# Experts' numbers, the first long list's rows and their preparation one step sooner, in a kernel of attention and two expert layers

## Chip, core and metric

One Trainium2 chip, one core. The metric is the device time of one execution in microseconds (us). An execution was also profiled; all rows below come from that one.

## What is computed

Clustered attention, then two expert layers on its output. The change lies in the first expert layer:

```
logits = x @ w_gate;  noisy = logits + log1p(exp(x @ w_noise)) * noise
top2 = two largest of 8 experts per token;  top2_w = softmax over the two
for e in range(8):
    for k in range(2):
        mask = top2[:, k] == e
        h = maximum(x[mask] @ w1[e], 0)
        out[mask] += top2_w[mask, k] * (h @ w2[e])
```

There are 1536 tokens of 512 numbers; w1 is 512 x 1024 and w2 is 1024 x 512 for each expert. All is float32 in the reference.

## The kernel before, in words

**Lists and jobs.** While attention runs, the tokens of every expert are written by indexed DMA into a list in HBM (`xg`). Experts 0 and 1 have two short lists each (256 rows, 240 of them used), one for each half of the batch; experts 2 to 7 have one long list each. Ten jobs work these lists off: jobs 0 and 1 are the short lists of the first half, jobs 2 to 7 the long lists from the fullest to the emptiest, jobs 8 and 9 the short lists of the second half. Which expert stands behind job 2 is known only at run time: `Dp.ranks`, called in step 6, sorts the six experts on VectorE (DVE) and leaves their numbers in `permi` (line 793).

**Steps.** A job has 8 steps, one for each 128 of the 1024 hidden numbers, so there are 80 steps; step s is job s // 8. Job 2, the first long list, begins with step 16. For step s:

- `load_w(s)` (lines 949 to 956): one DMA of 512 KB, issued by SyncE (SP), brings the weights of the step into one of four places `WR[s % 4]`.
- `split_hi(s)` (line 959) on ScalarE (ACT) writes the rounded weights to `ring`; `split_lo(s)` (lines 961 to 968) writes what the rounding left, on DVE. In steps 13 to 15 DVE does the first half (line 966) and GpSimd (POOL) the second (line 968). There are three places in `ring`, so `split_hi(s)` waits until TensorE (PE) has done `second(s - 3)`.
- `first(s)` (line 1061): 12 matmuls, over the rounded weights times both parts of the rows, and the rest times the rounded rows. The third matmul is the first that reads what `split_lo` wrote. Then ACT (line 1066) and DVE (line 1067) take the result out as `H`, again in two parts.
- `second(s)` (line 1102, for long lists `second_t`, line 1129): the product with w2. It reads both parts of `H`.

**Rows of a job.** `load_x(j)` (lines 970 to 998) issues four DMAs for the rows (line 982) and a few for the weights of the tokens (lines 994 and 996). For a long list their addresses come from the expert's number, which `load_perm` (line 945) reads from `permi` into registers of SP, six reads for six experts. `prep_t` (line 1016, DVE) turns half a list's rows, `prep_h` (line 1023, ACT) rounds them, and `prep_l` (line 1029, DVE for job 2) keeps the rest. Job 2 is done in two halves.

**Order of the work.** The loop at lines 1841 to 1919 writes out the order of every queue by hand; each engine, and SP, does its instructions in that order. Step s issues, in this order: at s == LX the experts' numbers (`load_perm`), then `load_w(s + 5)`, at s == LX also `load_x(2)`; then `first(s + 1)`, `second(s)`, `split_hi(s + 3)` and `split_lo(s + 3)`, and the preparations that the table `prep` has for the step. In steps 12 to 15 (`soon`) the preparations stand ahead of the two splits, in all others behind them. In step 15, `second(15)` comes ahead of `first(16)`.

`PREP[j] = (s, n, engines)` gives the step in which the turning of the first part of job j begins, in how many parts it is done, and on which engine `prep_l` runs; `PH` and `PL` (1 and 1) say how many steps later `prep_h` and `prep_l` of a part follow. Below, hi 13, lo 13, first 13, second 13 and H 13 are the splits, matmuls and hidden numbers of step 13, w 13 is its DMA, and x 2 are the rows of job 2.

The lines of the loop that set SP's order:

```
if s == LX:
    while todo:
        gap(1000, 1000)
    M1.load_perm()
if 4 + len(SP) <= s + 5 < ns:
    M1.load_w(s + 5)
if s == LX:
    M1.load_x(2)
```

Of the kernel before, what the change touches and what calls it, by code (L numbers as in the profile page):

```python
# [44 lines left out]


OV = 24
PREP = {2: (12, 2, "dd"), 4: (2, 3, "ppp"), 8: (3, 2, "dd"), 9: (8, 2, "dd")}
LOADS = {-16: ("b0",), -14: ("a0",), -12: ("a1",), -10: ("a2",), -8: ("a3",), -6: ("x0", "x2"), -5: ("x4", "b2"), -4: ("b3",), -3: ("c0", "c1")}
B4, B5, B6 = 6, 6, 3  # L50
X9 = 57
# [1464 lines left out]
def body(tc, qk, q2, k2, v2, cent, wgn, noise, w12, phi, v12, out):  # L1516
    nc = tc.nc
    with ExitStack() as ctx:
# [152 lines left out]
        for i in range(Dp.NFILL):  # L1671
            at(ends, 2 * (i // 4) + 3, Dp.fill, i)

        LX = 9
        todo = []
        gates = [Dp.gate(q, *x) for q, x in enumerate(((0, 6), (6, 3), (9, 3)))]

# [154 lines left out]
        for j in range(2, len(M1.jobs)):  # L1832
            s, n, eng = PREP[j if j in PREP else 4]
            if j > 2:
# [6 lines left out]
        for s in range(ns):  # L1841
            j, f = M1.steps[s]
# [8 lines that stand above are left out]
# [127 lines left out]
```

## Time and profile before

| what | us |
|---|---|
| median of 3 runs | 622.95 |
| the 3 runs | 622.3, 622.95, 626.76 |
| the profiled execution, its time | 620.13 |
| its span, first to last instruction | 618.3 |

The span is what the views below show; 1.83 us of the profiled execution lie around it. Steps 0 to 15 run from about 234 to 289 us of the span, job 2 begins at 289.45 us. A row of the timeline gives the start, the duration, engine and line, operation and tiles, and in brackets how long the engine was idle before it and what ended that. SPq is SyncE's queue.

### The profile page before, as it was taken

What the parts mean: (1) busy time and instruction counts of PE and PEld (TensorE: products, weight loads), DVE (VectorE), ACT (ScalarE), POOL (GpSimd) and SP (SyncE); (2) the same over time, 40 slices, a digit from 0 to 9 for tenths busy, and PEclk for the clock granted to TensorE, in tenths of its full rate; (3) what the DMA queues carried; (4) which work ended last, traced back from release to release, by engine and by line L of the source; (5) the groups of instructions that cost most, each with busy time, mean ns of one, the idle gap of its engine ahead of it and who ended that gap; (6) DMA issues with size and microseconds to landing.
All of it is one profiled execution on the core that took longest, in us unless ns stands there. A gap on an engine that the chain in (4) does not pass through costs nothing. (4 is left out here: it accounts for less than half of the span.)

```text
span 618.3 us, 11612 instructions
## 1 busy us (share of the span) xinstructions
PE 595.7 (96%) x4241; PEld 480.5 (78%) x4241; DVE 419.3 (68%) x841; ACT 322.0 (52%) x467; POOL 292.5 (47%) x267
## 2 busy tenths in 40 slices
PE   8999999999999999798999999999999999997996
PEld 6666767666677668587999999999999888874544
DVE  6875788676776388466554958769595977644533
ACT  5877667676676663255344363644646375532002
POOL 3998788787989851634030160432616044220100
PEclk9999999999999999899999999999999999999999
DMA  8262474552357683788935559899997979989985
GB/s 326 74 234 77 149 278 162 214 190 107 129 180 250 225 256 143 251 184 251 193 102 143 153 122 228 352 207 337 285 308 160 299 204 345 308 267 335 426 364 204
DMA packets 59084, 139.43 MB, mean 225 GB/s; under 512 B 11504, under 2 KB 27056, under 8 KB 56976
## 3 DMA queue, kind: packets, MB, share of 16 engines
q1 hardware_dynamic: 53168, 125.31, 60.2%
q0 software_dynamic: 5856, 13.36, 10.2%
q8 instruction: 34, 0.56, 0.4%
q14 instruction: 26, 0.21, 0.1%
HBM read 108.18 MB, written 28.35 MB: 221 GB/s over the span
## 5 line engine op out<-in xcount | busy, mean ns | idle before, releaser
L966 DVE TENSOR_TENSOR ring<-wr,ring 128x1024 fp32r<-128x1024 f32 (+1 forms) x77 | 92.6, 1203 | 62.1 <-ACT ring L959 61.0
L959 ACT ACTIVATE ring<-wr 128x1024 fp32r<-128x1024 f32 x77 | 81.4, 1059 | 78.3 <-PE py L1129 47.3
L1129 PE MATMUL py<-H,ring 128*128 128x448 f32 (+5 forms) x480 | 97.7, 352 | 0.0
L1129 PEld LDWEIGHTS py<-H,ring 128*128 128x128 f32 x480 | 88.6, 188 | 2.6
L352 DVE TENSOR_REDUCE mp<-pmx 128x1 f32<-128x512 f32 x96 | 63.7, 684 | 12.7 <-PE pmx L347 12.3
L1066 ACT ACTIVATE H<-ph 128x240 fp32r<-128x240 f32 (+6 forms) x80 | 36.4, 455 | 68.7 <-PE ph L1061 56.2
L395 ACT ACTIVATE pts<-psc 128x768 f32<-128x768 f32 x72 | 57.9, 812 | 26.6 <-PE psc L391 22.8
L1061 PE MATMUL ph<-XS1a,ring 128*128 128x240 f32 (+3 forms) x288 | 67.9, 326 | 0.0
L1102 PE MATMUL py<-ring,H 128*128 128x512 f32 (+1 forms) x246 | 64.0, 398 | 2.4 <-DVE H L1067 1.3
L1061 PE MATMUL ph<-XS0a,ring 128*128 128x432 f32 (+3 forms) x252 | 63.8, 337 | 0.1
L1152 POOL DMA_INDIRECT x2acc<-y,mdi x20 | 33.4, 1668 | 61.4 <-ACT y L1171 25.5
L1067 DVE SCALAR_TENSOR_TENSOR H<-ph,H 128x240 fp32r<-128x240 f32 (+6 forms) x80 | 40.8, 510 | 24.9 <-ACT H L1066 17.2
L1102 PEld LDWEIGHTS py<-ring,H 128*128 128x128 f32 (+1 forms) x246 | 42.4, 183 | 12.4 <-DVE H L1067 2.5
L408 PE MATMUL pav<-pts,vt 128*64 128x384 f32 x288 | 51.7, 492 | 0.0
L428 POOL TENSOR_TENSOR psa<-psa,pts 128x768 f32<-128x768 f32 x27 | 49.7, 1840 | 3.5 <-ACT pts L395 1.9
L1061 PEld LDWEIGHTS ph<-XS1a,ring 128*128 128x128 f32 x288 | 47.8, 188 | 2.1 <-DVE ring L966 0.2
L1029 POOL TENSOR_TENSOR XS0b<-xr,XS0a 128x512 fp32r<-128x512 f32 (+1 forms) x9 | 17.0, 1888 | 67.9 <-ACT XS0a L1023 67.9
L1061 PE MATMUL ph<-XS0b,ring 128*128 128x240 f32 (+3 forms) x192 | 46.2, 312 | 1.2 <-DVE ring L966 0.8
L1061 PE MATMUL ph<-XS1b,ring 128*128 128x240 f32 (+3 forms) x192 | 46.3, 314 | 0.1
L1061 PEld LDWEIGHTS ph<-XS0a,ring 128*128 128x128 f32 x252 | 44.2, 195 | 1.8 <-issue 0.5
L1029 POOL TENSOR_TENSOR XS1b<-xr,XS1a 128x512 fp32r<-128x512 f32 (+1 forms) x6 | 11.4, 1906 | 54.5 <-ACT XS1a L1023 54.5
L408 PEld LDWEIGHTS pav<-pts,vt 128*64 128x64 f32 x288 | 19.2, 136 | 23.1 <-issue 21.1
(377 smaller groups left out, 1205.0 us busy)
## 6 DMA issues: line engine op xcount, KB each, us to landing
wr<-in_w SPq DMA_DIRECT2D x80, 512.0 KB
v<-in_v SPq DMA_DIRECT2D x9, 2048.0 KB
xg<-xr SPq DMA_DIRECT2D x14, 516.0 KB
wr<-in_qk SPq DMA_DIRECT2D x8, 768.0 KB
early<-in_q SPq DMA_DIRECT2D x8, 768.0 KB
early<-in_k SPq DMA_DIRECT2D x8, 768.0 KB
x2acc<-xr SPq DMA_DIRECT2D x8, 512.0 KB
vt<-in_v SPq DMA_DIRECT2D x8, 384.0 KB
```

The source lines that it names most:

```text
L352: nc.vector.tensor_reduce(mp[:, 0, col:col + 1], ps, axis=AX.X, op=OP.max)
L395: nc.scalar.activation(pt, ps[:, :, :384], AF.Exp, scale=SCALE)
L408: nc.tensor.matmul(self.avp[p, qh][64 * hh:64 * hh + 64, :384], self.vt[p][:, hh, kc, :], pt[:, hh, :], start=(kc == 0), stop=(kc == 5))
L428: eng.tensor_tensor(s, s, pt.pop((p, t)), op=OP.add)
L959: self.nc.scalar.activation(self.ring[s][0], self.wr[s], AF.Copy)
L966: nc.vector.tensor_tensor(lo[:, :n], wr[:, :n], f32(hi)[:, :n], op=OP.subtract)
L1061: nc.tensor.matmul(ph[:, :u], a[:, 128 * c:128 * c + 128], x[:, c, :u], start=(c == 0 and i == 0), stop=(c == 3 and i == 2))
L1066: nc.scalar.activation(HH[:, :u], ph[:, :u], AF.Relu)
L1067: nc.vector.scalar_tensor_tensor(HL[:, :u], ph[:, :u], 0.0, f32(HH)[:, :u], op0=OP.max, op1=OP.subtract)
L1102: nc.tensor.matmul(py, x, y, start=(f == 0 and i == 0), stop=(f == NF - 1 and i == 2))
L1129: nc.tensor.matmul(py[:, :w], a[:, k], x[:, :w], start=(f == 0 and i == 0), stop=(f == NF - 1 and i == 2))
L1152: st = nc.gpsimd.indirect_dma_start(out=out, out_offset=bass.IndirectOffsetOnAxis(ap=di, axis=0), in_=y, in_offset=None, compute_op=OP.add)
```

## The change

`LX` goes from 9 to 8: the loop over `todo`, `load_perm` and `load_x(2)` move from step 9 to step 8. `PREP[2]` begins with step 11 and not 12: the turning of job 2's halves is issued in steps 11 and 12, `prep_h` and `prep_l` in steps 12 and 13. Since step 11 does not belong to `soon`, the first turning now stands behind the splits of step 14, not ahead of those of step 15.

```
-PREP = {2: (12, 2, "dd"), 4: (2, 3, "ppp"), 8: (3, 2, "dd"), 9: (8, 2, "dd")}
+PREP = {2: (11, 2, "dd"), 4: (2, 3, "ppp"), 8: (3, 2, "dd"), 9: (8, 2, "dd")}
...
-        LX = 9
+        LX = 8
```

## Rows read from the trace of the kernel before

**Rows 1.** The page, part 1: busy us, share of the span, instructions.
```profile
PE 595.7 (96%) x4241; PEld 480.5 (78%) x4241; DVE 419.3 (68%) x841; ACT 322.0 (52%) x467; POOL 292.5 (47%) x267
```

**Rows 2.** Waits of PE, 275 to 289.5 us: total, times, longest.
```profile
PE py L1102 <- DVE H L1067: 1.3, 1, 1.3
PE ph L1061 <- ACT ring L959: 0.4, 1, 0.4
```

**Rows 3.** Timeline of PE: second 12, second 13, first 15, second 14, first 16.
```profile
278.45 1.55 PE L1102 MATMUL py<-ring,H 128*128 128x512 f32 x6
...
281.18 1.56 PE L1102 MATMUL py<-ring,H 128*128 128x512 f32 x6
...
283.86 1.39 PE L1061 MATMUL ph<-XS0b,ring 128*128 128x240 f32 x10 [0.24 <-DVE ring L966]
285.08 2.02 PE L1102 MATMUL py<-ring,H 128*128 128x512 f32 x8
...
289.45 0.36 PE L1061 MATMUL ph<-XS1a,ring 128*128 128x448 f32 x1
```

**Rows 4.** Busy time of the engines, 289.5 to 550 us, clock, DMA.
```profile
289.50:550.00 260.50, 260.20 (x1417) 245.81 (x1416) 181.29 (x277) 129.68 (x190) 77.48 (x70) 1.00 0.83 240
```

**Rows 5.** Timeline of ACT: hi 13, hi 14, hi 15, H 14, first prep_h.
```profile
274.57 1.06 ACT L959 ACTIVATE ring<-wr 128x1024 fp32r<-128x1024 f32 x1 [1.02 <-PE py L1102]
...
277.31 1.06 ACT L959 ACTIVATE ring<-wr 128x1024 fp32r<-128x1024 f32 x1 [1.02 <-PE py L1102]
...
282.02 1.06 ACT L959 ACTIVATE ring<-wr 128x1024 fp32r<-128x1024 f32 x1 [3.00 <-DMA wr<-in_w]
282.98 0.35 ACT L1066 ACTIVATE H<-ph 128x240 fp32r<-128x240 f32 x1
283.23 0.94 ACT L1023 ACTIVATE XS1a<-xr 128x896 fp32r<-128x896 f32 x1
```

**Rows 6.** Line 945, SP's reads: ns min/median/max, first and last start.
```profile
L945 SPq TENSOR_LOAD <-permi x6: 263/274/786, 266.9 to 268.7; - x6
```

**Rows 7.** Timeline of SP: w 13, w 14, x 2, w 15.
```profile
264.65 0.33 SPq L955 DMA_DIRECT2D wr<-in_w  x1
...
269.59 0.34 SPq L955 DMA_DIRECT2D wr<-in_w  x1
270.23 3.05 SPq L982 DMA_DIRECT2D xr<-xg  x4
...
276.70 0.52 SPq L955 DMA_DIRECT2D wr<-in_w  x1
```

**Rows 8.** Timeline of DVE: permi, turning, lo 15, prep_l, lo 16, prep_l.
```profile
266.69 0.17 DVE L793 CAST permi<-perm 128x6 int32<-128x6 f32 x1
...
280.65 1.11 DVE L1016 STREAM_TRANSPOSE xr<-xr 128x896 f32<-128x896 f32 x1 [1.20 <-DMA xr<-xg]
283.11 0.69 DVE L966 TENSOR_TENSOR ring<-wr,ring 128x512 fp32r<-128x512 f32 x1 [1.34 <-ACT ring L959]
...
284.21 1.70 DVE L1029 TENSOR_TENSOR XS1b<-xr,XS1a 128x896 fp32r<-128x896 f32 x1
...
286.86 1.18 DVE L966 TENSOR_TENSOR ring<-wr,ring 128x1024 fp32r<-128x1024 f32 x1
...
288.29 1.07 DVE L1029 TENSOR_TENSOR XS1b<-xr,XS1a 128x896 fp32r<-128x896 f32 x1
```

**Rows 9.** DMA queue 1, 269.5 to 276 us: packets, MB, share.
```profile
q1 hardware_dynamic: 817, 0.86, 54.1%
```

**Rows 10.** DMA queue 1, 280.9 to 286 us.
```profile
q1 hardware_dynamic: 455, 1.61, 82.0%
```

**Rows 11.** Timeline of POOL: the second half of lo 15.
```profile
283.15 1.80 POOL L968 TENSOR_TENSOR ring<-wr,ring 128x512 fp32r<-128x512 f32 x1 [2.91 <-ACT ring L959]
```

**Rows 12.** Busy time by stretch, as rows 4: an earlier idle stretch, half clock.
```profile
251.80:254.70 2.90, 0.00 (x1) 0.00 (x0) 0.00 (x0) 0.39 (x2) 2.10 (x3) 1.00 0.95 355
255.85:259.27 3.42, 3.42 (x15) 3.02 (x13) 1.69 (x2) 0.35 (x1) 2.91 (x2) 0.50 0.61 165
```

## Prediction, made before the changed kernel was run

> **What bounds the kernel now.** I read the page first: PE is busy for 96% of the span [rows 1], so a change pays only where PE stands still, and costs wherever it makes PE stand still. Then the waits of PE in the steps that the change touches. Between 275 and 289.5 us PE waits 1.3 us for H 15, which DVE delivers late, and 0.4 us for hi 15 [rows 2]. The timeline of PE gives the whole loss [rows 3]: second 12 and second 13 begin 2.73 us apart, which is a step without a wait. From second 12 at 278.45 us three such steps would bring first 16 to 286.6 us; it begins at 289.45 us. So 2.8 us are to be had here and no more, 0.46% of the run. Next the stretch behind it: from 289.5 to 550 us PE is busy for 260.20 of 260.50 us [rows 4]. It follows that a microsecond lost or won before first 16 is not made up later; it goes through to the end.
>
> Why the loss is there: hi 15 waited 3.00 us for its weights, until 282.02 us [rows 5], because SP issued w 15 only behind the rows x 2, at 276.70 us [rows 7]. Then DVE had the turning and `prep_l` of job 2 between the splits, so that H 15 was late.
>
> **SP: what moves, and past what.** The change moves three things in SP's order. Before, it is w 13, reads of `permi`, w 14, x 2, w 15. After, it is reads of `permi`, w 13, x 2, w 14, w 15. The question is what the reads wait for. DVE writes `permi` at 266.69 us, for 0.17 us [rows 8]; the first of the six reads starts at 266.9 us and the last at 268.7 us [rows 6]. They already start the moment the numbers exist. `Dp.ranks` stays in step 6, so the reads start at 266.9 us after the change as well, and w 14's present slot at 269.59 us is the first one behind them. This is the core of my forecast: the rows cannot go out sooner, since SP already waited for the numbers. Only the two weight DMAs that stood between or ahead now stand behind.
>
> Slot by slot [rows 7]:
> - w 13 goes out at 269.59 us and not at 264.65 us: 4.9 us later.
> - x 2 goes out from 270.23 us, as now. Its four DMAs and three small ones take SP until w 15's slot.
> - w 14 goes out at 276.70 us and not at 269.59 us: 7.1 us later.
> - w 15 follows directly, much as now.
>
> The bytes and their order in the queue are the same but for one name, so I read the landings from the slots.
>
> **Wait for w 13.** What left at 269.59 us was in by about 276 us: until then queue 1 moved 0.86 MB, the 0.52 MB of the weights and a third of the rows [rows 9]. It cannot have been later than 277.31 us, since hi 14 began then, released by PE and not by a DMA [rows 5]. hi 13 now begins at 274.57 us, so it waits 1.5 us (between 0 and 2.7). From the start of a late hi to the second that follows its first takes 285.08 - 282.02 = 3.06 us [rows 3, 5]. So second 12 begins at 276.1 + 3.1 = 279.2 us and not at 278.45 us: 0.7 us late.
>
> **Wait for w 14.** What leaves at 276.70 us behind the rows lets hi start at 282.02 us [rows 5]. Now hi 14 starts at 277.31 us; after, at 282.0 us. Second 13 then begins at 282.0 + 3.1 = 285.1 us and not at 281.18 us [rows 3]: 3.9 us late. The 0.7 us of w 13 lie inside this, as do all its bounds. The bounds of this term: not before the rows themselves are in, 280.65 us, when the first turning stops waiting for them [rows 8], which is 1.4 us less; and I see no reason for more than half a microsecond above.
>
> ACT works in order, and H 13 stands behind hi 14 as H 14 stands behind hi 15 now (282.02, then 282.98 us) [rows 5]. It ends soon enough, since first 14 has to come first.
>
> **What goes, and what takes its place.** The wait for w 15 goes. Landing behind w 14, it is in by about 283.5 us: in the stretch after the rows queue 1 moves 1.61 MB in 5.1 us, 1.6 us for each 0.52 MB [rows 10]. The intended gain, a DVE free for H 15, does not come, for the preparation now falls into the late stretch. DVE's order from lo 14 on is lo 14, turning, H 13, `prep_l`, turning, lo 15, H 14, `prep_l`, lo 16, H 15. With the durations of [rows 5, 8]: lo 14 ends at 283.8 us as lo 15 does now; turning 1.11, to 284.9 us; `prep_h` 0.94 on ACT, to 285.9 us, and behind it hi 15, to 286.9 us; `prep_l` 1.70, to 287.6 us; turning 1.11, to 288.7 us; lo 15 0.69, to 289.3 us (0.1 us of starting in the sums). PE has done second 13 by 286.5 us and waits for lo 15. From the end of lo 15 to second 14 takes 285.08 - 283.80 = 1.28 us, so second 14 begins at 290.6 us. Second 14 and second 15 take 2.73 us, as a first and a second do, and first 16 begins at 293.3 us. H 15 is just in time: after lo 15, H 14 about 0.4 (0.35 on ACT [rows 5]), `prep_l` 1.07, lo 16 1.18 bring DVE to 292.0 us, and second 15 needs the result about 292.4 us.
>
> Unknown is the price of a `prep_l`: 1.70 us beside POOL's half of lo 15 (283.15 us, 1.80 us) [rows 11], 1.07 us without it [rows 8]. I take 1.70 for the first and 1.07 for the second, as in the profile; the other way round is 0.6 us less or more. The Trainium skill (SBUF — State Buffer, SBUF: two separate sides) says that DVE with two inputs in SBUF and a reading GpSimd lock each other out, and that whichever starts first keeps the port. By that rule the first `prep_l`, now ahead of POOL, would take 1.07 us, and lo 15 would wait for POOL until about 288.8 us and end at 289.5 us; the sum would be 0.2 us higher. The two rows agree with it.
>
> **Sum.** First 16 begins at 293.3 us and not at 289.45 us: 3.9 us later. The other instructions are as many as before and do the same work: POOL's halves and the two turnings end in time or are in the sum; the loop over `todo` has nothing left by step 8 that PE waits for. The profiled execution took 620.13 us, so 624.0 us. It lies 2.8 us below the median of the runs, 622.95 us; on that, 626.9 us. With the bounds added up (1.4 for the landing and 0.6 for `prep_l` below, 0.5 and 0.6 above) this case alone spans 624.9 to 628.0 us.
>
> **Rivals.**
> 1. *Faster: the rows do go out sooner.* Then w 14 and w 15 are in time, DVE turns the rows while it is idle, and all of 2.8 us is won: 620.2 us; if only the wait for H 15 goes, 621.6 us. For it speaks that DVE has room in steps 9 to 11. Against it stand the reads at 266.9 us. It decides at this point: from the start of the reads to w 14 lie 9.8 us of SP's time (266.9 to 276.70), and 5.3 us to its landing, so the reads would have to start before 262.2 us for hi 14 to begin at 277.31 us, 4.7 us sooner than `permi` exists.
> 2. *Slower still: PE's clock falls.* Waiting for hi 14 (280.6 to 283.1 us) and for lo 15 (from 287.4 us on), PE stands still for 2.5 and 1.9 us. Before, after 2.90 us without a matmul, the granted clock was 0.50, 1.2 GHz, for 3.42 us [rows 12]; that much work then takes 1.7 us longer. After the first idle it would lie beside the wait for lo 15 and cost nothing; after the second it costs 1.7 us: 628.6 us. Shorter idle times speak against it. The Trainium skill (TensorE: Matmul & The Clock Gate, What's actually happening) says that the lower clock is the resting state and only activity lifts it; the trace agrees with its 0.50.
> 3. *The weights pass the rows.* If w 14 moved beside x 2 rather than behind it, it would be in by about 279.5 us, x 2 some 1.5 us later, and the loss would be about 2 us: 624.9 us. Against it: now w 15 is let in just after the rows are [rows 5, 8].
>
> That the change does not do what it says is my forecast: `load_x(2)` is issued one step sooner in the program, but at the same time.
>
> **How the numbers follow.** Forecast 0.6, rival 1 0.1, rival 2 0.17, rival 3 0.13. A measurement tells about 1% from no change, 6.2 us. Slower by more (above 629.2 us): 0.03 beyond the forecast's own span, and 0.10 of rival 2 with its share of the same bounds, 0.13 in all. Faster by more: no case reaches 616.7 us; 0.02 for what I do not see. The range runs from 622.0 us, above rival 1, to 630.5 us, which holds rival 2 with its bounds above (628.6 + 1.1 = 629.7 us) and a little for what the sum overlooks.
>
> **What would show it.** Right: the reads still start at about 266.9 us, with w 13 behind them; ACT waits for weights ahead of hi 13 and, for about 4 us, ahead of hi 14; x 2 starts at about 270.2 us; PE waits for lo 15; first 16 begins near 293.3 us. Wrong: reads well before 266 us, no wait ahead of hi 14, or first 16 at or before 289.5 us; or a stretch behind it that makes the loss up.

## Result, and the profile after

The changed kernel takes 626.33 us, median of 20 runs (624.22 to 627.5); the kernel before, beside it, 622.33 us (621.06 to 628.48, 20 runs). The ratio is 1.0053, 95% interval 1.0039 to 1.0068. The medians lie 4.0 us apart; the ratio, which is not that of the medians, stands for 3.3 us (2.4 to 4.2). The forecast was 3.9 us slower.

The profiled execution took 626.65 us, 6.52 us more than that of before, which lay 2.2 us under its own median. So the profile has to be read from a place that the change doesn't touch. First the waits of PE in it, between 250 and 264 us:

```profile
PE py L1102 <- issue: 3.8, 1, 3.8
PE py L1102 <- ACT H L1066: 2.0, 1, 2.0
```

The kernel before waits at the same line, 4.0 us in two pieces (2.9 and 1.1):

```profile
PE py L1102 <- issue: 4.0, 2, 2.9
```

This early stall lies ahead of the change's first instruction, and it was longer here. PE's granted clock was also 0.50 twice around it, from 255.76 and from 262.58 us for 3.41 us each, and before only once [rows 12]. All this moves what comes behind: `permi` is written at 269.41 us and not at 266.69 us [rows 8], 2.72 us later.

```profile
269.41 0.23 DVE L793 CAST permi<-perm 128x6 int32<-128x6 f32 x1
```

Of the 6.63 us by which first 16 is later (296.08 and 289.45 us), 2.72 were there before the change could act, and 3.9 are left for the change.

SP's reads in the profile after, line 945 (ns min/median/max, first and last start), answer to [rows 6]:

```profile
L945 SPq TENSOR_LOAD <-permi x6: 267/278/571, 269.7 to 271.5; - x6
```

They start 0.3 us after `permi` begins to be written; before, it was 0.2 us. SP's timeline after, w 12 to w 15, answers to [rows 7]:

```profile
264.46 0.33 SPq L955 DMA_DIRECT2D wr<-in_w  x1
...
272.18 0.34 SPq L955 DMA_DIRECT2D wr<-in_w  x1
272.82 2.83 SPq L982 DMA_DIRECT2D xr<-xg  x4
275.92 0.87 SPq L994 DMA_DIRECT2D mt<-xg  x1
277.00 2.57 SPq L996 DMA_DIRECT2D mt<-xg  x2
279.68 0.53 SPq L955 DMA_DIRECT2D wr<-in_w  x1
280.29 0.38 SPq L955 DMA_DIRECT2D wr<-in_w  x1
```

The rows x 2 left at 272.82 us, 3.41 us after `permi`; before, it was 270.23 - 266.69 = 3.54 us. `load_x(2)` was moved a whole step, and counted from `permi` the rows left at the same time. w 13 now stands behind the reads and w 14 behind the rows. What that does on ACT (answers to [rows 5]; hi 13, hi 14, first `prep_h`, hi 15):

```profile
279.39 1.06 ACT L959 ACTIVATE ring<-wr 128x1024 fp32r<-128x1024 f32 x1 [3.06 <-DMA wr<-in_w]
...
285.35 1.06 ACT L959 ACTIVATE ring<-wr 128x1024 fp32r<-128x1024 f32 x1 [4.65 <-DMA wr<-in_w]
...
288.19 0.95 ACT L1023 ACTIVATE XS1a<-xr 128x896 fp32r<-128x896 f32 x1 [1.52 <-DVE xr L1016]
289.05 1.05 ACT L959 ACTIVATE ring<-wr 128x1024 fp32r<-128x1024 f32 x1
```

ACT waited once for weights before (3.00 us, hi 15); now it waits twice, 3.06 and 4.65 us, and hi 15 no more. On DVE the preparation of job 2 follows the late lo 14 (answers to [rows 8]: lo 14, turning, `prep_l`, turning, lo 15):

```profile
286.44 0.69 DVE L966 TENSOR_TENSOR ring<-wr,ring 128x512 fp32r<-128x512 f32 x1 [4.95 <-ACT ring L959]
287.05 1.11 DVE L1016 STREAM_TRANSPOSE xr<-xr 128x896 f32<-128x896 f32 x1
...
289.17 1.09 DVE L1029 TENSOR_TENSOR XS1b<-xr,XS1a 128x896 fp32r<-128x896 f32 x1 [0.72 <-ACT XS1a L1023]
290.18 1.10 DVE L1016 STREAM_TRANSPOSE xr<-xr 128x896 f32<-128x896 f32 x1
291.21 0.80 DVE L966 TENSOR_TENSOR ring<-wr,ring 128x512 fp32r<-128x512 f32 x1
```

DVE stood idle for 4.95 us and then had all of it at once. The turning no longer waits for rows: it begins as lo 14 ends, so they are in by then. PE's waits between 275 us and first 16 (answers to [rows 2]):

```profile
PE ph L1061 <- ACT ring L959: 2.9, 2, 2.4
PE ph L1061 <- DVE ring L966: 0.9, 2, 0.6
```

The wait for H 15 (1.3 us before) is gone. In its place stand longer waits for hi and lo. PE's timeline after has the largest, ahead of first 14, then the one for lo 15, and first 16 (answers to [rows 3]):

```profile
286.46 3.22 PE L1061 MATMUL ph<-XS0b,ring 128*128 128x240 f32 x12 [2.44 <-ACT ring L959]
...
292.06 1.39 PE L1061 MATMUL ph<-XS0b,ring 128*128 128x240 f32 x10 [0.62 <-DVE ring L966]
...
296.08 0.36 PE L1061 MATMUL ph<-XS1a,ring 128*128 128x448 f32 x1
```

In this profile nothing is made up behind first 16 (328.8 us to the end of the span, as before). Behind 275 us the clock fell once (stretches as in [rows 4, 12]):

```profile
286.48:289.89 3.41, 3.41 (x13) 3.12 (x14) 2.69 (x4) 1.89 (x3) 1.79 (x1) 0.50 0.51 175
296.05:556.50 260.45, 260.09 (x1418) 245.79 (x1416) 181.46 (x277) 129.68 (x190) 76.55 (x70) 1.00 0.83 239
```

### The profile page after: what moved, and what is told of

Its sections match the earlier page's. It is cut to its first block, busy times and chain, and to the rows that moved or that the text cites. A ratio compares the mean times of both kernels' runs of the same rounds, so it can differ in the third digit from the quotient of the medians.

```text
span 624.9 us, 11614 instructions
## 1 busy us (share of the span) xinstructions
PE 598.5 (96%) x4241; PEld 483.0 (77%) x4241; DVE 420.4 (67%) x841; ACT 321.7 (51%) x467; POOL 290.2 (46%) x267
## 5 line engine op out<-in xcount | busy, mean ns | idle before, releaser
L1152 POOL DMA_INDIRECT x2acc<-y,mdi x20 | 32.0, 1602 | 64.9 <-ACT y L1171 28.8
L1067 DVE SCALAR_TENSOR_TENSOR H<-ph,H 128x240 fp32r<-128x240 f32 (+6 forms) x80 | 40.8, 510 | 26.7 <-ACT H L1066 21.1
L1061 PE MATMUL ph<-XS0b,ring 128*128 128x240 f32 (+3 forms) x192 | 48.4, 326 | 4.1 <-ACT ring L959 2.9
L1061 PEld LDWEIGHTS ph<-XS0b,ring 128*128 128x128 f32 x192 | 31.9, 201 | 6.9 <-ACT ring L959 3.8
```

Source lines behind the costliest of these rows:

```text
L1061: nc.tensor.matmul(ph[:, :u], a[:, 128 * c:128 * c + 128], x[:, c, :u], start=(c == 0 and i == 0), stop=(c == 3 and i == 2))
L1067: nc.vector.scalar_tensor_tensor(HL[:, :u], ph[:, :u], 0.0, f32(HH)[:, :u], op0=OP.max, op1=OP.subtract)
L1152: st = nc.gpsimd.indirect_dma_start(out=out, out_offset=bass.IndirectOffsetOnAxis(ap=di, axis=0), in_=y, in_offset=None, compute_op=OP.add)
```

## Experiments

Three sets of runs, each with the kernel before beside it. The median of that kernel was 615.11, 620.08 and 622.49 us in them, so only ratios are compared across sets. In profiles of the first set the early stall was missing and `permi` existed at about 254 to 260 us.

**The load alone and the preparation alone.** First the load, twice:

```
-        LX = 9
+        LX = 8
```

> LX = 8 alone, the turning left in steps 12 and 13. My theory (w 14 waits behind the rows x 2 because the reads of permi are pinned): hi 14 waits for its weights as in the changed kernel, about 4 to 4.7 us, but lo 15 no longer waits behind a whole preparation, so about half of the loss is left: some 2 us over before, 624.3 us. Rival (it is the place of the turning in DVE's order that costs): as before, 622.3 us, within 0.7 us.

Measured: ratio 1.0018 (1.0002 to 1.0034), 616.07 us.

> LX = 8 alone once more, now beside the changed kernel. Theory (the wait for w 14 and the place of the turning each cost a part, and the parts add up): hi 14 waits as in the changed kernel, but DVE has lo 15 out about 2 us sooner: ratio 1.0015 to 1.004, at least 1 us under the changed kernel. Rival (the wait for the weights is the whole loss, the turning only fills it): as the changed kernel, within 0.7 us.

Measured: ratio 1.0045 (1.0026 to 1.0063), 624.29 us, beside the changed kernel's 1.0057 (1.0034 to 1.0079), 625.71 us. hi 14 in the timeline of ACT, in the first and the second of the two:

```profile
275.86 1.06 ACT L959 ACTIVATE ring<-wr 128x1024 fp32r<-128x1024 f32 x1 [4.09 <-DMA wr<-in_w]
```
```profile
283.67 1.06 ACT L959 ACTIVATE ring<-wr 128x1024 fp32r<-128x1024 f32 x1 [4.02 <-DMA wr<-in_w]
```

The load alone brings the wait for w 14 in both sets, and costs. Whether the moved turning adds to it the times of the second of these sets do not settle: the medians differ by 1.4 us, and the intervals overlap widely. The profiles of that set say that it does: first 16 comes 23.7 us behind `permi` with the load alone and 26.7 us with both, against 22.8 us in the profile before. But that one execution of the load alone took 627.23 us, 2.9 us more than its median, and spent 332.2 us from first 16 on, against 328.85 us in the profile before. So where the load alone loses its time was not found. Then the preparation:

```
-PREP = {2: (12, 2, "dd"), ...}
+PREP = {2: (11, 2, "dd"), ...}
```

> PREP[2] from step 11 alone, LX left at 9. My theory: no wait of hi 13 or hi 14 for weights; the first turning waits on DVE for the rows until about 280.7 us of the profile before and holds H 13 and lo 15 back by 1 to 2 us: about 1 us over before, 623.3 us. Rival (the place of the turning costs it all): 4 us over before, 626.3 us. If earlier preparation were a gain by itself: 621 us or less.

Measured: 1.0034 (1.0018 to 1.005), 617.22 us: 2.1 us slower where I expected 1. The first turning in DVE's timeline:

```profile
276.32 1.11 DVE L1016 STREAM_TRANSPOSE xr<-xr 128x896 f32<-128x896 f32 x1 [2.52 <-DMA xr<-xg]
277.36 0.37 DVE L1067 SCALAR_TENSOR_TENSOR H<-ph,H 128x240 fp32r<-128x240 f32 x1
```

It waits 2.52 us for its rows, and H 13 stands behind it; PE then waits 2.1 us for H 13 and 1.4 us for lo 15. Part of the cost is PE's clock, which was 0.50 from 280.6 to 287.4 us: the ten matmuls of first 15 took 2.49 us, second 14 and second 15 4.68 us, where the changed kernel has 1.39 and 2.96 us at the full clock (next section). How much of the 2.1 us that is stays open, since the kernel before was not profiled in this set. By their times, each half of the change costs by itself. The preparation alone needs rows that are not there, and the load cannot bring them sooner.

**What holds the rows back.** `Dp.ranks` two steps sooner, with the rest as in the changed kernel:

```
-        LX = 8
+        LX, RK = 8, 4
...
             if s == 6:
                 assert len(todo) <= 6
+            elif s == RK:
                 Dp.ranks(M1.mo, M1.perm, M1.permi)
```

> The changed kernel with Dp.ranks issued in step 4 and not in step 6, so that permi exists long before SP asks for it. My theory (the reads' wait for permi is what turns the gain into a loss): the reads follow w 12 at once, the rows x 2 go out about 4 us sooner, w 14 by about 272.6 us on the clock of the profile before, hi 14 waits under 1 us, H 15 is in time: 1 to 2.8 us under before, 619.5 to 621.3 us, which is 5 to 7 us under the changed kernel. Rival (the rows ahead of w 14 cost that much wherever they stand): 625 us or more.

Measured: 1.0008 (0.999 to 1.0026), 615.16 us, and not 1 to 2.8 us under before. A miss. One of SP's waits from 255 to 270 us says why:

```profile
SPq L982 <- DMA xg<-x,idx: 3.5, 1, 3.5
```

With `permi` out of the way, the first row DMA (line 982) waited 3.5 us for the last indexed DMA that writes the lists into `xg`, and left at 264.04 us. In that set a second event held the rows, right behind the first. While SP waited, w 14 stood behind the rows with its place free, and hi 14 waited 5.77 us. I took from this that without the early stall the lists set the time and with it `permi` does: the stall delays `permi` by some 7 us (260 and 267 us), but the last indexed DMA of the lists was issued at 257.8 us here and at 259.4 us in the profile before. That was tried where the stall was there:

> The changed kernel with Dp.ranks in step 4, beside the changed kernel. If PE has its early stall here (permi of the changed kernel at 266 us or later): the reads come early and the rows leave behind w 13 at about 265 us and not at 270.2 us, hi 14 waits under 2 us, ratio 0.996 to 1.001, 3 us or more under the changed kernel. If the stall is missing (permi of the changed kernel near 260 us): the landing of the lists in HBM holds the rows at about 264 us, hi 14 waits 5 us or more, ratio 1.000 to 1.004. Rival (permi has no part in it): as the changed kernel in both cases.

Measured: 0.997 (0.9952 to 0.9988), 620.76 us, against 625.71 us of the changed kernel in the same set: 4.95 us. The stall was there (5.6 us of PE's waits). The reads, then the rows on SP, then hi 14 on ACT, then PE's wait from 275 us to first 16:

```profile
L945 SPq TENSOR_LOAD <-permi x6: 261/274/501, 264.9 to 266.8; - x6
```
```profile
268.18 1.99 SPq L982 DMA_DIRECT2D xr<-xg  x4
```
```profile
280.25 1.06 ACT L959 ACTIVATE ring<-wr 128x1024 fp32r<-128x1024 f32 x1 [1.60 <-DMA wr<-in_w]
```
```profile
PE ph L1061 <- DVE ring L966: 1.4, 1, 1.4
```

The reads no longer wait for `permi` (261.96 us) but start right behind w 12 (264.54 us). The rows leave at 268.18 us, though not at 265 us as expected: w 13, ahead of them, waits for its place until 267.54 us. hi 14 waits 1.60 us. This is the version that beats both kernels of this case, in a set with the stall.

The kernel before with `Dp.ranks` in step 4, LX 9 and PREP[2] 12:

> The kernel before with Dp.ranks issued in step 4 alone. SP's reads end before w 14's place is free, so w 14 and x 2 go out 0.3 to 0.6 us sooner and the wait for w 15 shrinks by as much; the preparation stays where it is. Expected 0 to 0.6 us under before, 621.7 to 622.3 us. If it gains as much as the changed kernel with ranks in step 4, then the sooner load and preparation are worth nothing.

Measured: 0.9967 (0.9949 to 0.9986), 613.46 us.

> The kernel before with Dp.ranks in step 4, on which the best of the runs so far rests (0.9967). If the gain is the earlier reads, which let w 14 and the rows leave as soon as their place and the lists allow: ratio 0.996 to 0.999 again. If it was chance of that set of runs, or holds only without the early stall: 0.999 to 1.002.

Measured: 0.9994 (0.9979 to 1.0008), 622.27 us. So the sooner numbers alone gain 0.3% in one set and nothing in the other; over both it stays open. In the set of the 4.95 us they gain nothing by themselves, so the gain there comes from the sooner numbers and the sooner load together.

**What w 14 waits for.** The changed kernel again, beside three others:

> The changed kernel once more, beside the experiments. In the first four runs the early stall of PE (two idle times between 251 and 260 us) was missing and permi existed at about 260 us and not at 266.7 us, so the reads are no longer the last thing that holds the rows back: there the landing of the list's rows in HBM at about 264 us is. Theory now (the rows stand ahead of w 14 and nothing makes them leave a step sooner): hi 14 waits 4 to 5 us for its weights also without that stall, and the loss is 2.5 to 4 us, ratio 1.004 to 1.0065. Rival (the loss came only from the late permi of the first profile): ratio under 1.002.

Measured: 1.0072 (1.0054 to 1.0089), 624.89 us. The expectation tied this to a missing stall; it was there. `permi` existed when it did in the profile before, which makes this profile the best measure of my numbers (next section). Then w 14 ahead of the rows:

```
-            if 4 + len(SP) <= s + 5 < ns:
+            if 4 + len(SP) <= s + 5 < ns and s != LX + 1:
                 M1.load_w(s + 5)
             if s == LX:
+                M1.load_w(s + 6)
                 M1.load_x(2)
```

> The changed kernel with w 14 issued ahead of the rows x 2: reads, w 13, w 14, x 2, w 15. Theory (w 14 behind the rows is the loss): hi 14 waits under 2 us, and what is left is the place of the turning, as in the run with the preparation alone: ratio 1.002 to 1.0035, clearly under the changed kernel beside it. Rival (w 13 behind the reads, or the turning alone, is the loss): as the changed kernel, within 0.7 us.

Measured: 1.0081 (1.0065 to 1.0098), 625.42 us: no better than the changed kernel. Another miss. hi 14 on ACT, then DVE's turning, then PE's second 13:

```profile
277.52 1.06 ACT L959 ACTIVATE ring<-wr 128x1024 fp32r<-128x1024 f32 x1 [0.47 <-DVE ring L966]
```
```profile
282.26 1.11 DVE L1016 STREAM_TRANSPOSE xr<-xr 128x896 f32<-128x896 f32 x1 [2.95 <-DMA xr<-xg]
```
```profile
283.72 1.20 PE L1102 MATMUL py<-ring,H 128*128 128x512 f32 x4 [1.53 <-DVE H L1067]
```

The wait for w 14 is gone, as the theory said, but the rows then land 1.6 us after 280.65 us [rows 8], and the turning that was moved to step 11 holds H 13 until they do. The two waits are alternatives: whichever of w 14 and x 2 goes second, something in step 11 needs it. So w 14's place in the queue is not the whole cause.

That the loss is as large as the changed kernel's has a second reason, which the times alone hide: the lower clock that rival 2 had priced. Behind the waits for H 13 (1.53 us) and hi 15 (0.44 us) PE's clock fell to 0.50 for 6.8 us, and the wait for lo 15 (1.12 us) lies beside only a part of that. The stretch as in [rows 12], then first 15's ten matmuls, then second 14 with second 15:

```profile
285.10:291.92 6.82, 5.44 (x18) 4.60 (x19) 5.06 (x7) 2.73 (x5) 1.30 (x2) 0.50 0.51 177
```
```profile
287.26 2.49 PE L1061 MATMUL ph<-XS0b,ring 128*128 128x240 f32 x10 [1.12 <-DVE ring L966]
289.55 4.03 PE L1102 MATMUL py<-ring,H 128*128 128x512 f32 x12
```

In the changed kernel of this set the same work took 1.39 and 2.96 us (next section), at the full clock. So an estimate from these rows is that 2.2 us of this version's loss are the clock. From second 10 to first 16 it took 20.60 us, against 16.47 us before, so about 2 us of the loss are left without the clock, which is what the expectation had for the turning alone. No run has this order at the full clock throughout.

Then only the small DMAs of `load_x(2)` (token weights, lines 994 and 996) behind w 15, called in step LX + 2:

```
-        for a in range(4):
+        for a in () if late else range(4):
...
+        if j == 2 and late is None:
+            self.xr[j] = (xr, xT, None)
+            return
...
             if s == LX:
                 M1.load_x(2)
+            if s == LX + 2:
+                M1.load_x(2, True)
```

> The changed kernel with the three small DMAs of x 2 (the token weights) issued behind w 15 and not ahead of w 14. If SP's time for them (3.4 us from the first small DMA to w 14) and their 512 packets are part of the wait: w 14 is issued 3.4 us sooner, hi 14 begins 1.5 to 2.5 us sooner, the loss falls by that, ratio 1.001 to 1.003. Rival (the rows' bytes in the queue alone set it, SP's slot does not matter): within 0.7 us of the changed kernel.

Measured: 1.007 (1.0053 to 1.0087), 625.38 us. The rival holds for w 14: SP issued w 14 at 273.39 us and not at 277.79 us (the changed kernel in this set), 4.4 us sooner, and hi 14 began at 282.63 us and not at 282.95 us, 0.32 us sooner. The two, w 14 on SP and hi 14 on ACT:

```profile
273.39 1.31 SPq L955 DMA_DIRECT2D wr<-in_w  x1
```
```profile
282.63 1.06 ACT L959 ACTIVATE ring<-wr 128x1024 fp32r<-128x1024 f32 x1 [4.35 <-DMA wr<-in_w]
```

So what is in the queue ahead of w 14, the rows, sets its landing, and not SP's time. In this profile first 16 even came 1.24 us later than in the changed kernel's (294.93 and 293.69 us). The clock fell later there, behind a wait of 1.41 us for lo 15, and first 15's ten matmuls took 2.43 us, second 14 with second 15 3.54 us:

```profile
289.40:292.81 3.41, 3.41 (x13) 3.13 (x14) 2.81 (x4) 1.47 (x3) 0.00 (x0) 0.50 0.43 155
```

Last, on the kernel before with `Dp.ranks` in step 4, the rows issued in pieces and the splits of step 12 ahead of the turning:

```
-        for a in range(4):
+        for a in {None: range(4), 0: (0, 1), 1: (2, 3), 2: ()}[part]:
...
-            if s == LX:
-                M1.load_x(2)
+            if LX <= s < LX + 3:
+                M1.load_x(2, s - LX)
...
-            soon = NREG * NF - 4 <= s < NREG * NF
+            soon = NREG * NF - 3 <= s < NREG * NF
```

> The kernel before with Dp.ranks in step 4 (ratio 0.9967 before), the four row DMAs of x 2 issued two and two behind w 14 and w 15, the small ones behind w 16, and in step 12 the splits ahead of the turning. Theory (a weight DMA must not stand behind the whole of the rows): hi 15 waits under 2.5 us and not 4.65 us, H 15 is in time, 1 to 2 us better than ranks in step 4 alone: ratio 0.9935 to 0.9955. Rival (the same bytes delay some weight all the same, or the rows come too late for the turning): 0.9967 or more.

Measured: 1.0063 (1.0039 to 1.0088), 624.7 us: a miss, slower than before and not faster. hi 15 waited 1.68 us, as wanted, but the turning started at 286.04 us, PE waited 0.7 us for ACT's part of H 15 and 1.6 us for DVE's, and the clock was 0.50 for 3.4 us behind that.

The third set had the changed kernel too:

> The changed kernel as the measure for the three beside it. Expected ratio 1.005 to 1.008; hi 13 and hi 14 wait for their weights, 3 to 4 and 4 to 5 us.

Measured: 1.0057 (1.0034 to 1.0079), 625.71 us; hi 13 waited 2.28 us, less than expected, and hi 14 5.50 us.

## Why the prediction was right, step by step

In the second profile of the changed kernel (first of its set above) `permi` was written at 266.67 us, 0.02 us from where it was before, so that my times can be held against it directly. `permi`, its reads, its SP (w 13; w 14 with w 15), its ACT (hi 13, hi 14), its PE, and the stretch at the lower clock:

```profile
266.67 0.17 DVE L793 CAST permi<-perm 128x6 int32<-128x6 f32 x1
```
```profile
L945 SPq TENSOR_LOAD <-permi x6: 263/274/786, 266.9 to 268.7; - x6
```
```profile
269.58 0.34 SPq L955 DMA_DIRECT2D wr<-in_w  x1
...
277.79 1.00 SPq L955 DMA_DIRECT2D wr<-in_w  x2
```
```profile
277.14 1.06 ACT L959 ACTIVATE ring<-wr 128x1024 fp32r<-128x1024 f32 x1 [3.60 <-DMA wr<-in_w]
...
282.95 1.06 ACT L959 ACTIVATE ring<-wr 128x1024 fp32r<-128x1024 f32 x1 [4.50 <-DMA wr<-in_w]
```
```profile
280.20 1.57 PE L1102 MATMUL py<-ring,H 128*128 128x512 f32 x6
284.06 0.50 PE L1061 MATMUL ph<-XS0b,ring 128*128 128x240 f32 x2 [2.29 <-ACT ring L959]
284.79 2.31 PE L1061 MATMUL ph<-XS0b,ring 128*128 128x240 f32 x10 [0.23 <-DVE ring L966]
286.90 2.27 PE L1102 MATMUL py<-ring,H 128*128 128x512 f32 x6
...
289.66 1.39 PE L1061 MATMUL ph<-XS0b,ring 128*128 128x240 f32 x10 [0.27 <-DVE ring L966]
290.88 2.96 PE L1102 MATMUL py<-ring,H 128*128 128x512 f32 x12
293.69 0.36 PE L1061 MATMUL ph<-XS1a,ring 128*128 128x448 f32 x1
```
```profile
285.00:288.40 3.40, 3.40 (x14) 3.08 (x14) 2.68 (x4) 2.16 (x3) 1.51 (x2) 0.50 0.48 154
```

| step | forecast, us | measured, us |
|---|---|---|
| reads start | 266.9 | 266.9 |
| w 13 issued | 269.59 | 269.58 |
| w 14 issued | 276.70 | 277.79 |
| hi 13 starts | 276.1 | 277.14 |
| second 12 starts | 279.2 | 280.20 |
| hi 14 starts | 282.0 | 282.95 |
| second 13 starts | 285.1 | 286.90 |
| second 14 starts | 290.6 | 290.88 |
| first 16 starts | 293.3 | 293.69 |

**SP's order** was right: the reads pinned the rows. Shown by the run with `Dp.ranks` in step 4 in the third set, 4.95 us faster than the changed kernel, while the same move did nothing for the kernel before in that set (0.9994). What I did not see is that a second pin, the landing of the lists, lies close behind; it showed itself in the first set.

**The waits for w 13 and w 14** were each about 1 us too short in my sum; w 14's 282.95 us lies above the half microsecond that I gave it upward. Second 13 was later still, 1.8 us, because PE's clock was 0.50 from about 285.0 us on: the ten matmuls of first 14 took 2.31 us and not 1.39 us. The lower clock did not reach first 16, since PE had to wait for lo 15 anyway, in the end only 0.27 us; the later hi 14 did, through lo 15. Rival 2 had said that a fall behind the wait for hi 14 would lie beside the wait for lo 15, at no cost; there it lay.

**The preparation in the late stretch** was the term that gave some of it back: the first `prep_l` took 1.09 us, and I had taken 1.70. In the first profile it started at 289.17 us, ahead of POOL's half of lo 15, which came 1.00 us later, when `prep_l` was all but over. My own times had said so: POOL's half waits for hi 15, which I had end at 286.9 us, 1.0 us after the start of `prep_l`; the price without POOL was the one to take. The Trainium skill (SBUF — State Buffer, SBUF: two separate sides) says that whichever starts first gets the shared port. The two overlap by only 0.1 us, so this `prep_l` hardly tests it. The wait of lo 15 for POOL that I had worked out by that rule was small: in the second profile lo 15 began 0.24 us before POOL's half ended (288.81 and 289.05 us) and took 0.80 us and not 0.69, in keeping with the rule. So two terms missed by about 1 and 0.6 us with opposite signs, and the sum was closer than its terms, which is luck.

**What lies behind first 16.** I read it only to 550 us [rows 4] and took it that nothing is made up. In the second profile first 16 is 4.24 us later than before, but the execution only 3.47 us (623.60 and 620.13 us). The other 0.8 us were made up behind 550 us, in part at PE's wait for the rows of `x2acc`, 1.8 us before and 1.4 us here.

**The rivals.** Rival 1 needed the reads about 4.7 us sooner; with `Dp.ranks` in step 4 `permi` was 7.4 us sooner than in the changed kernel of that set (261.96 and 269.31 us), the reads 4.6 us (264.9 and 269.5 us), and the sign turned, as rival 1 said, to 0.3% faster, though not by all of its 2.8 us: hi 14 still waited 1.60 us. Rival 2's costly case, a lower clock behind the wait for lo 15, did not come in the changed kernel, but it did with w 14 ahead, with the small DMAs late and with the preparation alone. Rival 3, weights that pass the rows, is refuted for this order by the small DMAs put behind w 15: w 14, issued 4.4 us sooner, gained 0.32 us.

**Where the reason was too narrow.** I put the loss down to w 14 behind the rows. With w 14 ahead of them it was as large, though by the estimate above about half of that was the lower clock. What the runs show is that both are needed in step 11 as the changed kernel has it, hi 14 by the weights and the first turning by the rows, and the rows have no earlier start to make room for both. The size came out right because in the order that the change makes only one of the two waits is seen, and the lower clock lies beside another wait.

## What to carry to other kernels

Before a load is moved up in the program, look at what its issuing queue waited for: if the addresses, or the data to be loaded, come into being just ahead of it, it will leave at the same time, and only what it was moved past gets later. Then find the second event behind the first, for it will be the bound once the first is taken away. And look at both sides of a swap in a queue: what is put second is late, so ask of either order which consumer in program order stands behind the late one. When a version that should be faster is not, look at PE's clock in its trace before giving up the theory: beside another wait the lower clock cost nothing here, with none behind it an estimated 2.2 us.

## What was not expected of the hardware

**The early stall comes and goes.** PE's idle time at line 1102 between 250 and 264 us, with nothing changed ahead of it, was 4.0 us in the profile before, 5.8 us after, and 4.3 and 5.6 us in the changed kernel of the second and third set, while a profile of the first set (load alone) shows no wait above 0.4 us there. The first and the second set ran on the same chip, so it is not the chip that makes the difference. The medians of the kernel before differ with it: 615.11 us in the first set, 620.08 to 622.49 us in the others. That the stall makes this difference was not tested. What PE waits for there was not found; for its first part the profile names nothing ("issue").

**Waits of under 2.5 us were followed by the lower clock.** Before, the granted clock was 0.50 (1.2 GHz) after 2.90 us without a matmul [rows 12]. In the changed kernel it fell after idle times of 2.44 us (first profile) and 2.29 us (second), for 3.4 us each time, and with the load alone in the first set after 1.89 us. The length of one wait does not tell it: with the small DMAs late, the ten matmuls of first 14 behind a wait of 2.14 us took 1.39 us, as at the full clock, and the clock fell 5 us later, behind 1.41 us. In the changed kernel it cost nothing only because another wait lay behind it.
